# Nine fewer matmuls in the first batch of a sliding-window attention and mixer kernel

## The chip, the cores and the metric

One core of a Trainium2 chip. The metric is device time in microseconds (us) of one execution of the kernel.

## The reference

```python
scores = scale * np.matmul(q, k.transpose(0, 1, 3, 2))   # 8 batches, 8 heads, 576 tokens, 64 wide
rel = pos[:, None] - pos[None, :]
mask = (rel >= 0) & (rel < 64)                           # causal, window of 64
attn = softmax(np.where(mask, scores, -1e9))
x = np.matmul(attn, v)                                   # then (8, 576, 512)
h = x.T @ U @ V                                          # low-rank token mixing, rank 32
u = x + h.T
out = u + np.maximum(u @ w_ch1, 0.0) @ w_ch2             # channel MLP, 512 -> 2048 -> 512
```

## The kernel before

The attention of batch b + 1 is placed into slots between the MLP's matmuls of the chunk before, to keep TensorE without a pause (in the trace of before it is busy 219.98 of the 220.00 us from 60 to 280). Batch 0 has nothing to hide behind: its attention is the prologue, and its variant is called `spare`. There the mask is added before the scores by a matmul of the identity with a bias of 0 or -30000, and the scores are summed on top.

```python
def SC(j):                                   # scores of head pair j
    def f():
        if j not in sbank:
            masked(j)                        # spare: mask bias into both PSUM banks
        sc = sbank[j]
        banks = [sc[:, g, :] for g in range(2)]
        scores(banks, 0, j, 0, 0, 2)         # keys of block 0 with queries of blocks 0 and 1
        scores(banks, 0, j, 1, 0, 1)         # keys of block 1 with queries of block 0
        for u in range(1, NB - 1):
            scores(banks, u, j, u, u, 2 if u < NB - 2 else 1, last=(u >= NB - 3))
        ...                                  # exponential on ScalarE

opened = []
def idle_turns(n):                           # matmuls whose result nobody reads
    cols = P if opened else CH
    bank(1)
    for _ in range(n * (CH // cols)):
        nc.tensor.matmul(bank(0)[:, 0:cols], idle[:, 0:P], idle[:, 0:cols],
                         start=not opened, stop=not opened)
...
turn_over(62, 96)                            # warm-up: 62 unread matmuls of 96 columns
...
order = "K0 K1 B0 B1 Q0 Q1 S0 K2 S1 K3 B2 Q2 Q3 S2 B3 S3 L0 B4 S4 L1"
...                                          # B: mask bias, S: scores, L: first values
load_rest()
a["R"]()
shift_high(0, nc.scalar.copy, 2)
shift_low(0, nc.scalar.copy, 2)
a["idle"](1)
a["PV"][2]()                                 # values product that waits for GpSimd's copies of v
...
for f in [a["U"][NT - 1]] + a["X3"] + a["HT"]:
    f()                                      # psh of 256 columns, then hh; MLP (psA) follows
```

Names in the profile: `psA` and `psU` are the MLP's two products, `psh`/`hh` the low-rank one, `xr` and `xw` values products, `low` the first scores of a later batch, `kr`/`qr` loaded k and q, `kf`/`qf` transposed k and q, `vB` the copy of v shifted by 64 rows. From batch 2 on, k and q are transposed by DMA (SyncE's queue), five tiles of each.

The softmax here doesn't subtract the row's maximum and nothing guards it: scores larger than these inputs give would overflow.

## Time and profile before

| | before |
|---|---|
| median time, first 3 runs | 310.14 us (309.88 to 310.33) |
| span of the profiled run, granted clock | 308.6 us, 1.00 |
| TensorE busy | 302.1 us, 98% |
| first product of the MLP (psA) | 22.02 us |
| sixth instruction packet | 51.81 us |
| last transposed q of batch 2: lands, is used | 67.06, 67.59 us |

From psA on, TensorE is busy without a gap in this trace up to the last product: 11.98 of 12.00 us from 22 to 34, 26.00 of 26.00 from 34 to 60, 219.98 of 220.00 from 60 to 280, 25.07 of 25.07 from 280 to 305.07. So the span is psA's start, plus a fixed amount of work, plus whatever TensorE must wait for after psA. TensorE's position is compared instruction by instruction with this trace, and the difference is called its lead (negative: ahead of this trace). The page sums its chain up so:

```profile
PE 93%; DMA 3%; POOL 2%; issue 1%; DVE 0%; POOLq 0%
```

Two transposes of SyncE's queue, from its timeline in the kernel before (columns: start, length, engine, line, operation):

```profile
55.93 1.57 SPq L307 DMA_TRANSPOSE qf<-qr  x1
57.61 1.21 SPq L307 DMA_TRANSPOSE kf<-kr  x1
```

The second begins 0.11 us after the first ends (57.50 and 57.61). The first stays 1.57 us where its neighbours stay 1.21.

### The profile page before, as it was taken

The page shows a single profiled execution, that of the slowest core. Times are in us where ns is not written, and L with a number is a line of the kernel's source. Part 1 is how long each engine was busy: PE and PEld are TensorE (multiplying, and loading weights), DVE is VectorE, ACT ScalarE, POOL GpSimd, SP SyncE. Part 2 cuts the span into 40 slices and gives each one's busy share as a digit, 9 for nine tenths or more (in the row PEclk, how much of TensorE's full clock was granted, in tenths as well). Part 3 has the DMA queues.
Part 4 walks back from the last instruction along what each step waited for, and adds up shares of the span by engine and source line. Part 5 has one row for each costly group of instructions (what it writes and reads, how often), then busy time and mean ns, then how long its engine had stood idle before and what let it go on. Part 6 is the DMA issues. An engine that isn't in the chain of part 4 may idle for free.

```text
span 308.6 us, 6947 instructions
## 1 busy us (share of the span) xinstructions
PE 302.1 (98%) x2883; PEld 146.4 (47%) x2883; DVE 174.2 (56%) x336; ACT 106.0 (34%) x169; POOL 102.1 (33%) x136
## 2 busy tenths in 40 slices
PE   7989999999999999999999999999999999999995
PEld 7543454545445544454445444544454444444443
DVE  4585467537848763777467755766576542116012
ACT  2745670358008510552064205430443004101500
POOL 8693264195069519417541725000000000000000
PEclk9999999999999999999999999999999999999999
DMA  7999999999999999999999999955100464010011
GB/s 100 169 208 209 206 172 149 148 139 148 148 108 154 126 158 148 195 161 163 175 176 131 176 175 151 155 111 136 71 2 0 106 229 162 34 68 36 0 68 68
DMA packets 158671, 40.39 MB, mean 131 GB/s; under 512 B 147216, under 2 KB 153616, under 8 KB 158640
## 3 DMA queue, kind: packets, MB, share of 16 engines
q0 software_dynamic: 104720, 18.88, 84.8%
q1 hardware_dynamic: 53920, 21.08, 39.3%
q8 instruction: 22, 0.36, 0.5%
q14 instruction: 9, 0.07, 0.1%
HBM read 37.97 MB, written 9.44 MB: 154 GB/s over the span
## 4 chain that ended last, share of the span: by engine, by line
PE 93%; DMA 3%; POOL 2%; issue 1%; DVE 0%; POOLq 0%
PE psA L766 41%; PE psU L790 41%; DMA vA<-in_v_dram 3%; PE sc L348 3%; PE xw L410 2%; PE psv L661 1%; PE pshh L534 1%; PE tpg L284 0%; POOL qr L121 0%; PE low L348 0%; PE psh L534 0%; POOL vB L153 0%; PE tpu L695 0%; PE xr L410 0%; POOL kr L121 0%
## 5 line engine op out<-in xcount | busy, mean ns | idle before, releaser
L766 PE MATMUL psA<-uTc,w1b 128*128 128x512 bf16 (+1 forms) x580 | 131.0, 378 | 0.3 <-DVE uTc L636 0.3
L790 PE MATMUL psU<-w2b,c 128*128 128x512 bf16 (+2 forms) x592 | 128.4, 374 | 0.0
L790 PEld LDWEIGHTS <-c 128*128 128x128 bf16 x592 | 56.1, 98 | 66.4 <-issue 2.9
L766 PEld LDWEIGHTS <-w1b 128*128 128x128 bf16 x580 | 54.0, 98 | 64.4 <-issue 2.6
L778 ACT ACTIVATE c<-psA 128x512 bf16<-128x512 f32 x84 | 50.1, 597 | 80.5 <-PE psA L766 80.2
L776 DVE TENSOR_SCALAR c<-psA 128x512 bf16<-128x512 f32 x60 | 41.4, 690 | 38.5 <-PE psA L766 38.5
L803 DVE TENSOR_TENSOR osb<-psU,un 128x512 f32<-128x512 f32 (+2 forms) x29 | 19.5, 671 | 51.2 <-PE psU L790 51.2
L368 ACT ACTIVATE pts<-sc 128x1024 bf16<-128x1024 f32 x32 | 31.3, 1030 | 2.8 <-PE sc L348 2.8
L139 POOL DMA_DIRECT2D vA<-in_v_dram x32 | 28.3, 904 | 11.5 <-DMA w1b<-in_moe_w_ch_dram 3.0
L676 DVE TENSOR_TENSOR un<-psv,xs 128x512 bf16<-128x512 f32 (+3 forms) x48 | 25.8, 594 | 6.6 <-PE psv L661 6.5
L130 POOL DMA_DIRECT2D qr<-in_q_dram x30 | 26.6, 887 | 7.0 <-DMA w2b<-in_moe_w_ch_dram 2.9
L130 POOL DMA_DIRECT2D kr<-in_k_dram x30 | 26.3, 876 | 5.0 <-PE psA L766 2.0
L401 ACT ACTIVATE ptl<-low 128x256 bf16<-128x256 f32 x6 | 2.3, 383 | 64.9 <-PE high L348 64.9
L374 DVE TENSOR_TENSOR pts<-pts,maskA 128x1024 bf16<-128x1024 bf16 x28 | 19.0, 683 | 2.2 <-ACT pts L368 2.2
L501 DVE TENSOR_TENSOR xs<-xw,rcw 128x896 bf16<-128x896 f32 x14 | 15.3, 1092 | 0.5
L965 POOL COPY held<-qf 1x1 bf16<-1x1 bf16 x5 | 0.9, 178 | 44.2 <-DMA qf<-qr 44.2
L348 PEld LDWEIGHTS <-kf 64*64 64x64 bf16 x704 | 9.8, 107 | 7.6 <-issue 7.3
L348 PE MATMUL sc<-qf,kf 64*64 64x128 bf16 (+1 forms) x608 | 11.5, 212 | 0.5 <-DVE qf L301 0.3
L410 PEld LDWEIGHTS <-pts 128*64 128x64 bf16 x512 | 10.0, 110 | 3.7 <-issue 3.1
L139 POOL DMA_DIRECT2D vB<-in_v_dram x8 | 7.2, 896 | 5.6 <-DMA qr<-in_q_dram 2.4
L803 DVE TENSOR_TENSOR late<-psU,un 128x512 f32<-128x512 f32 x8 | 5.4, 686 | 6.1 <-PE psU L790 6.1
L410 PE MATMUL xw<-vA,pts 128*64 128x65 bf16 x217 | 8.5, 195 | 0.0
(125 smaller groups left out, 177.1 us busy)
## 6 DMA issues: line engine op xcount, KB each, us to landing
out_dram<-osb SPq DMA_DIRECT2D x27, 256.0 KB, 2.3
vA<-in_v_dram POOLq DMA_DIRECT2D x32, 128.0 KB, 9.6
kr<-in_k_dram POOLq DMA_DIRECT2D x24, 128.0 KB, 7.6
qr<-in_q_dram POOLq DMA_DIRECT2D x24, 128.0 KB, 7.5
w2b<-in_moe_w_ch_dram POOLq DMA_DIRECT2D x4, 512.0 KB, 15.6
out_dram<-late SPq DMA_DIRECT2D x8, 256.0 KB, 3.0
vB<-in_v_dram POOLq DMA_DIRECT2D x8, 128.0 KB, 11.3
w1b<-in_moe_w_ch_dram POOLq DMA_DIRECT2D x2, 512.0 KB, 10.9
```

The source lines that it names most:

```text
L130: nc.gpsimd.dma_start(out=dst[0:rows, t, :, :], in_=src[b, :, t * P : t * P + rows, :].rearrange("h p d -> p h d"),)
L139: nc.gpsimd.dma_start(out=dst[:, :, 0:D], in_=v[b, :, lo : lo + P, :].rearrange("h p d -> p h d"))
L348: nc.tensor.matmul(sc[g][r0 : r0 + W, col * W : (col + n) * W], keys_of(j, u, rs), queries_of(j, blk, n, rs), start=not spare, stop=last o ...
L368: nc.scalar.activation(out=dst, in_=sc[:], func=ACT.Exp, scale=scale)
L374: nc.vector.tensor_tensor(out=dst, in0=dst, in1=maskA.rearrange("p g n w -> p g (n w)"), op=ALU.mult)
L410: nc.tensor.matmul(dst, pts[:, h // 2, h % 2, blk, :] if blk < NB - 1 else ptl[:, h // 2, h % 2, :], rhs, start=True, stop=True,)
L676: nc.vector.tensor_tensor(out=u_tiles[g][rs, cs], in0=ps[0][n][rs], in1=x[rs, t, :, :].rearrange("p h d -> p (h d)")[:, cs], op=ALU.add,)
L766: nc.tensor.matmul(ps[i][:, ts.start * P : ts.stop * P], w1b[:, dc, i * P : (i + 1) * P], uTc[:, ts, dc, :], start=(dc == 0), stop=(dc == ...
L776: nc.vector.tensor_relu(out=c1[i][:], in_=ps[i][:])
L778: nc.scalar.activation(out=c1[i][:], in_=ps[i][:], func=ACT.Relu)
L790: nc.tensor.matmul(acc[t][:, lo:hi], c1[i][:, t * P : (t + 1) * P], w2b[:, i, lo:hi], start=(i == 0), stop=(i == NFC - 1),)
L803: nc.vector.tensor_tensor(out=osb[:, lo:hi], in0=acc[t][:, lo:hi], in1=u_tiles[g][:, lo:hi], op=ALU.add,)
```

## The change

Its intent: remove TensorE work from the prologue. The product of block 1's keys with block 0's queries is masked anyway: its columns hold -30000 from the bias, with or without it. It goes for batch 0 (two matmuls in each of four head pairs), and the unread matmul before the values product goes too.

```diff
                 scores(banks, 0, j, 0, 0, 2)
-                scores(banks, 0, j, 1, 0, 1)
+                if not spare:
+                    scores(banks, 0, j, 1, 0, 1)
...
-        opened = []
-
-        def idle_turns(n):
-            cols = P if opened else CH
-            ... (body cut)
         def XT(t, dcs):
             def f():
-                opened.append(t)
...
-            pcs["idle"] = idle_turns
...
     shift_low(0, nc.scalar.copy, 2)
-    a["idle"](1)
     a["PV"][2]()
```

More of the change, by code (lines that the diff above doesn't have):

```diff
@@ L590, in bank @@
             return ua[dc]
-        opened = []
-        def idle_turns(n):
-            cols = P if opened else CH
-            bank(1)
-            for _ in range(n * (CH // cols)):
-                nc.tensor.matmul(
-                    bank(0)[:, 0:cols],
-                    idle[:, 0:P],
-                    idle[:, 0:cols],
-                    start=not opened,
-                    stop=not opened,
-                )
         def XT(t, dcs):
             def f():
-                opened.append(t)
                 for dc in dcs:
```

## The prediction

> **What bounds the kernel now.** I read the page first. Its busy table and its chain that ended last say the same thing: TensorE.
>
> ```profile
> span 308.6 us, 6947 instructions
> PE 302.1 (98%) x2883; PEld 146.4 (47%) x2883; DVE 174.2 (56%) x336; ACT 106.0 (34%) x169; POOL 102.1 (33%) x136
> q8 instruction: 22, 0.36, 0.5%
> ```
>
> So anything that lets TensorE start its dense part earlier is worth its full length, unless something later waits; anything that shortens work before a wait is worth nothing. The nine removed matmuls all lie in batch 0, before the first product of the MLP (psA) at 22.02 us. I therefore asked for busy time by stretch: from 22 to 34 us TensorE is busy 11.98 of 12.00, from 34 to 60 it is 26.00 of 26.00, from 60 to 280 it is 219.98 of 220.00, each at a granted clock of 1.00. Before 22 us it has holes. The question is which of the holes swallow the saving. The chain in order of time, from 6 to 22 us, answers that:
>
> ```profile
> 5.29 0.88 POOL vA L139
> 6.17 8.05 DMA vA<-in_v_dram
> 14.22 0.05 issue
> 14.27 0.61 POOL vB L153
> 14.88 0.06 issue
> 14.94 0.62 POOL vB L150
> 15.56 0.06 issue
> 15.61 0.62 POOL vB L153
> 16.24 0.04 issue
> 16.28 0.45 PE xr L410 x16
> ...
> 19.53 0.32 PE psh L534 x2
> 19.85 0.31 issue
> 20.16 0.32 PE psh L543 x4
> 20.49 0.02 issue
> 20.51 0.43 DVE hh L575
> ```
>
> (Columns: start, length, what.) Until 16.28 us the chain is not TensorE at all: a load of v lands at 14.22, GpSimd makes three shifted copies of it, and only then may TensorE begin the values product of 16.28. After that TensorE carries the chain, with one hole named "issue", 19.85 to 20.16. The last view is TensorE's timeline around the removed idle matmul (L598) and that hole:
>
> ```profile
> 15.70 0.39 PE L598 MATMUL uam<-idle 128*128 128x512 bf16 x1
> 16.28 0.19 PE L410 MATMUL xr<-vB,pts 128*64 128x65 bf16 x1 [0.19 <-POOL vB L153]
> ...
> 20.16 0.29 PE L543 MATMUL psh<-xs,ub 128*32 128x256 bf16 x4 [0.31 <-issue]
> 20.99 0.39 PE L626 MATMUL uam<-vrep,hh 64*128 64x256 bf16 x4 [0.20 <-DVE hh L575]
> ```
>
> [...] a 512-column mask matmul is followed by its like after 0.22 us but by a 64-column transpose after 0.31 us, so a switch costs some 0.09 us, and L598 sits between two. [...] The page above has 22 instruction packets of 0.36 MB together, 16 KB each[...]; that matters below.
>
> **The change part by part.**
>
> 1. Scores. In each of four head pairs, two 64x64 matmuls go, with their weight loads. Eighteen matmuls of such a group take 0.35 us from their start to the next group's (9.60 to 9.95), so about 20 ns each: 8 x 20 = 0.16 us. Two groups stand before 11 us, two before 14.1 us. All are before the 16.28 wait, which a DMA landing and GpSimd set. ScalarE's exponentials may start 0.04 us earlier, but the third product's inputs and the v copies do not. On the path: 0.
> 2. The idle matmul: 0.22 us of streaming and two mode switches of 0.09 us, about 0.4 us. It also stands before 16.28. On the path: 0. The order of instructions shows that only its two waits go with it, and that the first transposing matmul into that PSUM bank now carries the wait for VectorE itself; that matmul runs at 16.66 and the wait was met by 15.70, so nothing new is waited for.
> 3. Nothing else moves: in ScalarE, VectorE, GpSimd and DMA queues the order and waits are the same. TensorE's stream is 18 rows shorter (nine loads, nine matmuls).
>
> By parts 1 and 2 the gain is 0 although about 0.55 us of TensorE work goes. Part 3 is where I expect what little there is. The hole before L543 has no cause in the data: its weight load waits for nothing and still starts only at 20.16, and the matmul's input from VectorE was signalled at 19.56 (semaphore records of the trace). By the 0.21 us that 512 columns take, it could have started at 19.68, so the hole is 0.48 us. In the trace an instruction packet moves from 17.78 to 18.72 us. I take the hole for the end of an instruction line that was late [...]; the profile does not say so, it is an inference. If so, the line ends at a fixed row, and 18 rows fewer before it move the end from the first weight load of L543 to the second product of L626. That product waits for VectorE anyway: with L543 at 19.68 the two halves of hh are cast from 20.03, the first signalled at about 20.46 instead of 20.95, and the late line, there at 20.16 or a little later, hides under it. Then psA starts at 22.02 - 0.48 = 21.54.
>
> What of 0.48 us survives? I compared landing times with first use. The second q load of batch 1 lands at 33.18 and is used at 33.93: enough. The fourth piece of w2b lands at 47.97 (issued at 36.01, 12.0 us to landing) and its first product starts at 48.29. With a few hundredths for the signal, TensorE can gain only 48.29 - 48.02 = 0.27 us there. Behind it nothing binds closer: the last transposed q of batch 2 lands at 67.06, used at 67.59. So if the hole moves, the gain is about 0.27 us; if not, 0.
>
> **Rivals.**
>
> - All removed work counts: 0.55 us, 309.6. For it: TensorE is 98% busy. Against it: the chain at 16.28 belongs to GpSimd and a load.
> - Nothing counts, the hole stays in front of L543 (it has another cause, or the late line is not at a fixed row): 310.1.
> - The hole moves but lands worse, say the instruction packet now comes later, or the first packet (10.83 us, 0.95 us long), behind which one of the sixteen shares of each v tile lands a microsecond late (13.15 against 12.18 for the rest), shifts relative to those loads. Later: plus 0.3, 310.4. If it moved out of the way of the loads, GpSimd's chain could start earlier, by up to a microsecond: 309.2. The packet would have to move by more than 2 us for that; 12 rows will not do it.
> - [...]
>
> **Range and chances.** I give the moved hole 60%, no effect 25%, the rest 15%. Around the best guess of 0.27 us that makes a mean gain close to 0.2 us: 310.14 - 0.2, so 309.9 us. Three runs of the kernel before span 309.88 to 310.33, so a median may sit 0.2 us off. The range 309.3 to 310.5 holds all but [...] the lucky DMA shift. 2% would be 6.2 us, more than ten times the removed work[...].
>
> **What would show it.** Right: the values product after GpSimd's copy still starts at about 16.28, now after a longer wait for GpSimd; the hole before the 256-column psh products is gone or below 0.1 us; hh is cast about 0.4 us earlier; psA starts near 21.5; a new wait of some 0.2 us for w2b appears near 48. Wrong: the 16.28 moves earlier (then TensorE's own work was on the path, or the v load landed earlier), the hole stays at 20.16, or a granted clock below 1.00 or 512-column matmuls longer than 0.39 us appear after 16 us.

The forecast's sum: 310.14 minus a mean gain close to 0.2 us (0.27 us for the moved hole, which had 60%) gives 309.9, with 309.3 to 310.5 around it. The granted clock was 0.999 to 1.00 in all five runs of the changed kernel.

A switch, or mode switch, is the step from one tile shape to another, and its 0.09 us is an estimate: the 0.31 us from the start of a 512-column mask matmul to that of a transpose (7.96 and 11.35 us in the trace of before) less the 0.22 us to one of its like. The removed 0.55 us is an estimate too, from 0.16 us for the score products and about 0.4 for the idle matmul (0.22 and two switches). An instruction line is the stretch of TensorE's rows that one instruction packet is taken to bring; that a hole stands at its end, at a fixed row, was an inference, which before_minus9 and before_minus4 test below. Why a line should be late is not shown.

## The result, and the profile after

| | before | after |
|---|---|---|
| median (range), 5 runs each | 310.31 us (309.88 to 310.58) | 310.59 us (310.28 to 310.91) |
| ratio after/before, 95% | | 1.0012 (0.9998 to 1.0026) |

A ratio is the mean time of one kernel's runs over that of the other's of the same rounds, so not quite the ratio of the medians quoted. The time of 310.59 is 0.09 us above the predicted range.

The page of the changed kernel: its span, its busy time, and the summary of its chain.

```profile
span 308.9 us, 6908 instructions
PE 299.5 (97%) x2853; PEld 145.7 (47%) x2874; DVE 175.4 (57%) x336; ACT 106.0 (34%) x169; POOL 102.3 (33%) x136
PE 90%; DMA 4%; POOL 2%; DVE 2%; issue 1%; POOLq 0%; SPq 0%
```

The counts hold a trap: the matmuls fall by 30 and the weight loads by 9. Nine were removed; the remaining 21 are matmul records that the trace lost, so the 2.6 us less of busy TensorE are mostly not real. What can be trusted is the chain: DMA and VectorE have taken 3% that TensorE had.

The chain in order of time, before the MLP (start, length, what; the lines answer to those that the prediction quotes):

```profile
15.80 0.62 POOL vB L153
16.43 0.04 issue
16.47 0.45 PE xr L411 x16
...
19.68 0.32 PE psh L535 x2
20.01 0.14 PE psh L544 x4
20.17 0.43 DVE hh L576
...
21.68 1.02 PE psA L751 x4
```

The values product still follows GpSimd's third copy, now 0.19 us later because the load of v landed at 14.41 instead of 14.22. But the "issue" line in front of the 256-column psh is gone, and psA starts at 21.68, 0.34 us ahead. That part went as predicted. Then the lead is lost. TensorE's waits list (us in total, times, longest) names where:

```profile
PE xr L411 <- POOL vB L153: 0.8, 1, 0.8
...
PE xw L411 <- DVE vB L153: 0.2, 1, 0.2
...
PE low L348 <- DMA qf<-qr: 0.2, 1, 0.2
```

The first is the predicted longer wait for GpSimd. The other two are new, and both lie behind psA:

1. At 67.5 us the first scores of batch 2 (`low`) wait for the last transposed q. It landed at 67.06 before and lands at 67.44 now, although TensorE arrives earlier. SyncE's timeline in the changed kernel shows where it was held up:

```profile
55.55 2.65 SPq L307 DMA_TRANSPOSE qf<-qr  x1
58.30 1.21 SPq L307 DMA_TRANSPOSE kf<-kr  x1
```

This transpose began 0.38 us earlier than before and stayed 2.65 us instead of 1.57, so the next begins 0.69 later. In the DMA records, the sixth instruction packet (16 KB) moves at 55.84, taking 1.57 us; before it moved at 51.81 in 0.97 us. Beside it, the last q load of batch 2 lands at 58.71 instead of 57.65; of its sixteen shares one came at 57.36, the other fifteen at 58.34 to 58.71. The lead shrinks from -0.34 to -0.11.

2. At 101 us a values product of batch 3 waits for VectorE's copy of v. In the chain of the changed kernel:

```profile
100.43 0.60 DVE c L761
101.03 0.93 DVE vB L153 x2
101.97 0.04 issue
102.01 0.39 PE xw L411 x13
```

The second of the two copies takes 0.80 us by its record; in the kernel before both together fitted into 0.52:

```profile
101.06 0.52 DVE L153 COPY vB<-vA 64x520 bf16<-64x520 bf16 x2
```

The lead goes from -0.11 to +0.26. Another 0.05 us slips in later: the last product starts at 305.38 against 305.07. The account of the trace closes: -0.34 + 0.23 + 0.37 + 0.05 = +0.31 us, which is the 0.3 by which the spans differ.

### The profile page after: what moved, and what is told of

It reads as the page before. It is cut to its first block, busy times and chain, and to the rows that moved or that the text cites. A ratio compares the mean times of both kernels' runs of the same rounds, so it can differ in the third digit from the quotient of the medians. Undisturbed runs are those within 1.5% of the kernel's fastest.

```text
span 308.9 us, 6908 instructions
## 1 busy us (share of the span) xinstructions
PE 299.5 (97%) x2853; PEld 145.7 (47%) x2874; DVE 175.4 (57%) x336; ACT 106.0 (34%) x169; POOL 102.3 (33%) x136
## 4 chain that ended last, share of the span: by engine, by line
PE 90%; DMA 4%; POOL 2%; DVE 2%; issue 1%; POOLq 0%; SPq 0%
PE psU L775 40%; PE psA L751 39%; DMA vA<-in_v_dram 3%; PE sc L348 3%; PE xw L411 2%; DMA qf<-qr 2%; PE psv L647 1%; PE pshh L535 1%; DVE c L761 1%; PE tpg L284 0%; POOL qr L121 0%; PE low L348 0%; PE psh L535 0%; POOL vB L153 0%; PE tpu L681 0%
## 5 line engine op out<-in xcount | busy, mean ns | idle before, releaser
L775 PE MATMUL psU<-w2b,c 128*128 128x512 bf16 (+2 forms) x573 | 126.9, 373 | 1.2 <-issue 0.3
```

The costliest lines, as they stand in the source:

```text
L775: nc.tensor.matmul(acc[t][:, lo:hi], c1[i][:, t * P : (t + 1) * P], w2b[:, i, lo:hi], start=(i == 0), stop=(i == NFC - 1),)
```

## The experiments

**The theory**: the shorter instruction stream moves the sixth instruction packet onto batch 2's last loads (this takes part of the lead), and the copy at 101 takes the rest. **Rivals**: the losses are chance, in both kernels alike; or the score products and the idle matmul matter for themselves, by their work or the waits they carried.

All traces side by side. "Packet" is the start of the sixth instruction packet, "q load" the landing of the last q load of batch 2, "qf" that of the last transposed q, "low" the start of its first use; "wait" the wait there; "last" the start of the last product. Rows are TensorE instructions, a weight load and a matmul each one. (That these packets carry TensorE's instructions is an inference: the trace of before holds 22 of them and 5766 loads and matmuls, 262 for each, and the stops found below under before_minus9 lie 256 rows apart.) The list of waits leaves out those under 0.15 us.

| trace | early rows | psA | packet | q load | qf | low | wait | last |
|---|---|---|---|---|---|---|---|---|
| before | 0 | 22.02 | 51.81 | 57.65 | 67.06 | 67.59 | - | 305.07 |
| before_again | 0 | 21.56 | 52.12 | 57.67 | 66.95 | 67.13 | - | 304.91 |
| idle_only | -2 | 21.59 | 51.90 | 57.20 | 66.42 | 67.22 | - | 305.00 |
| before_minus4 | -8 | 22.18 | 51.57 | 57.48 | 66.15 | 67.75 | - | 306.04 |
| scores_only | -16 | 21.66 | 55.85 | 58.37 | 67.17 | 67.38 | - | 305.20 |
| after | -18 | 21.68 | 55.84 | 58.71 | 67.44 | 67.49 | 0.2 | 305.38 |
| after_again | -18 | 21.80 | 55.89 | 59.06 | 68.26 | 68.30 | 0.6 | 305.98 |
| after_third | -18 | 21.64 | 55.84 | 58.80 | 68.01 | 68.05 | 0.8 | 306.12 |
| before_minus9 | -18 | 22.64 | 56.61 | 57.43 | 67.97 | 68.21 | - | 305.78 |
| after_plus9 | 0 | 22.28 | 51.88 | 57.37 | 66.67 | 67.86 | - | 306.41 |
| plus9_pv9 | 0 | 21.93 | 51.77 | 57.27 | 66.75 | 67.50 | - | 305.03 |
| after_late9 | -18, then 0 | 21.53 | 51.64 | 57.44 | 66.67 | 67.10 | - | 305.01 |
| late9_pv9 | -18, then 0 | 22.78 | 51.76 | 57.71 | 66.53 | 68.35 | - | 306.07 |
| late9_pv9_again | -18, then 0 | 21.51 | 51.64 | 57.55 | 67.08 | 67.27 | - | 305.10 |

### before_again: the kernel before, unchanged

> The kernel before, unchanged, traced a second time, to see what differs between two runs of one kernel. Theory (instruction line): the hole ahead of the 256-column psh products stands at about 20.2 us again, psA starts within 0.25 us of 22.0, and no product waits at 67.6 or 101.7 us. Rival (the later waits come and go by chance): a wait for the transposed q near 67.6 or for the DVE copy of v near 101.7 shows here too. Time ratio 1.000 within 0.001.

Measured: 310.06 us (309.81 to 310.61), ratio 0.998 (0.9961 to 0.9998) against other runs of the identical kernel in the same rounds, which came out at 310.64 (309.86 to 311.4). The interval leaves out 1 although nothing was changed: a difference of 0.2% is not resolved here, even where the interval says so. The trace is the more telling part. The hole before the 256-column psh is not there: psh starts at 19.64 and psA at 21.56. The kernel before has that head start by itself in this trace; of the two traces of the unchanged kernel one has the hole and one has not. And the copy of v at 101 cost this kernel 0.25 us too. VectorE's timeline of this run:

```profile
100.81 0.68 DVE L153 COPY vB<-vA 64x520 bf16<-64x520 bf16 x1
```

So the wait at 101 does not belong to the change.

### after_again and after_third: the changed kernel, unchanged

> The changed kernel, unchanged, traced a second time. Theory: no hole ahead of the psh products again, psA near 21.7, and the waits near 67.5 (transposed q) and 101.7 (DVE copy of v) are both there again, so that the end comes 0.2 to 0.4 us later than before; the first belongs to the sixth instruction packet falling at 55.8 instead of 51.8. Rival (chance): at least one of the two waits is missing and the span is then 0.2 to 0.7 us shorter. Time ratio 1.0005 to 1.0015 by the theory, 0.999 to 1.001 by chance.

> The changed kernel a third time, beside the two above on one chip. Theory: packet at 55.8, q load landing at 58.4 to 59.1, last product 305.2 or later, and time 0.2 to 0.6 us above after_late9. Rival: a third trace without the late q load, and a time that cannot be told from after_late9.

Measured: 310.69 us (310.42 to 311.18), ratio 0.9997 (0.9977 to 1.0016), and 310.74 us (310.24 to 311.32), ratio 1.0007 (0.999 to 1.0024). The wait at 67.5 is in both traces, longer than in the first. TensorE's waits lists, first of after_again, then of after_third:

```profile
PE low L348 <- DMA qf<-qr: 0.6, 1, 0.6
```

```profile
PE low L348 <- DMA qf<-qr: 0.8, 1, 0.8
```

With the packet at 55.84 to 55.89 in all three, the wait goes with the changed kernel in each of its traces, which chance would hardly do. Its size is not fixed (0.2 to 0.8 us), and none of it was won back by the end of these traces. But the traced executions of after_again and after_third (311.18 and 311.32 us) were the slowest of their six, so they are not typical of the kernel's time.

### scores_only and idle_only: each half of the change alone

```diff
  scores_only: kernel before, and
-                scores(banks, 0, j, 1, 0, 1)
+                if not spare:
+                    scores(banks, 0, j, 1, 0, 1)
  idle_only: kernel before, and
-    a["idle"](1)
```

> Only the eight score products go, the idle matmul stays: 16 rows fewer ahead of the psh products. Theory (instruction line at a fixed row): the line now ends inside the first HT pair, where VectorE is waited for anyway, so the hole ahead of the 256-column psh products is gone and psA starts near 21.6 to 21.8. Rival (the idle matmul's removal made the hole vanish[...]): the hole stays and psA starts near 22.0.

> Only the idle matmul goes, the score products stay: 2 rows fewer ahead of the psh products. Theory (line at a fixed row): the line ends one load and one product later, inside the group of four psh products, so three of the four wait as before, hh is cast as late as before, and psA starts near 22.0. Rival (the idle matmul was the cause): no hole, psA near 21.7.

Measured: scores_only 310.28 us (309.85 to 310.61), ratio 0.9985 (0.9967 to 1.0003); idle_only 310.69 us (310.21 to 311.42), ratio 1.0 (0.998 to 1.0019). In idle_only psA started at 21.59; I had expected about 22.0, the hole staying in front of psh. It was a miss, and before_again explains it: there was no hole to keep. The packets separate cleanly: 16 rows fewer put the sixth packet at 55.85 and the q load at 58.37, two rows fewer leave them at 51.90 and 57.20. In scores_only the last transposed q still came 0.21 us before its use, so no wait; at 67.17 it landed later than in any trace with the early packet (67.08 at most), and the margin is a matter of tenths. The times cannot rank the halves.

### before_minus9 and before_minus4: fewer rows, all products kept

To take rows away without touching the change, the warm-up was given fewer and wider matmuls, with nearly the same number of columns (62 x 96 = 5952, 53 x 112 = 5936, 58 x 102 = 5916).

```diff
  before_minus9: kernel before, and
-    turn_over(62, 96)
+    turn_over(53, 112)
  before_minus4: kernel before, and
-    turn_over(62, 96)
+    turn_over(58, 102)
```

> The kernel before with 53 warm-up matmuls of 112 columns in place of 62 of 96 (the same 5 us of warm-up): all nine products of the change stay, but TensorE's stream is 18 rows shorter ahead of everything, as in the changed kernel. Theory (row count moves the sixth instruction packet into the last q load of batch 2): the packet falls at 55.8 +- 0.2 us instead of 52, that q load lands at 58.4 to 59.1 instead of 57.2 to 57.7, the last transposed q at 67.2 to 68.3, and the end comes as late as in the changed kernel: last product at 305.2 to 306.0, time 310.3 to 310.8. Rival (the removed products themselves, or chance): packet at 52, last product at 304.9 to 305.1, time 310.0 to 310.3.

> The kernel before with 58 warm-up matmuls of 102 columns: 8 rows fewer. Where the step lies between 2 rows (packet at 51.9) and 16 rows (55.85). Theory: the packet falls either near 52 or near 55.8, or between, later the fewer rows[...]. Rival: no relation between the row count and the packet.

Measured: before_minus9 310.98 us (310.58 to 311.47), ratio 1.0028 (1.0016 to 1.0041); before_minus4 one run, 311.26 us. Eighteen rows fewer moved the packet to 56.61 (expected 55.8), without any of the change's edits; the q load of batch 2 was on time though (57.43), which I had not expected, and yet the last transposed q came at 67.97, since two transposes stayed long in SyncE's queue (1.71 and 1.95 us). Eight rows fewer left it at 51.57. So the number of rows moves the packet, and the way from the packet to the transposed q is not always the q load.

The loss of time has its place elsewhere, and it is the clearest picture of a stop that the data do not explain. TensorE's timeline in before_minus9:

```profile
13.77 0.34 PE L348 MATMUL sc<-qf,kf 64*64 64x128 bf16 x10
15.03 0.30 PE L348 MATMUL sc<-qf,kf 64*64 64x128 bf16 x8 [0.92 <-issue]
```

In the middle of a group of 18 equal products, with nothing in the data to wait for, TensorE stops for 0.92 us. In before_minus4 it stops in the same score group for 0.74, after five products instead of ten. Counted in rows, with TensorE's few drain and semaphore rows, both stop after the same one, row 449 of its stream, whatever stands there; the hole of the first trace of before comes after row 705, exactly 256 rows further. TensorE went on 2.4 to 2.65 us after the start of the instruction packet before it (17.78 and 20.16; 12.40 and 15.03; 11.86 and 14.51). That fits the prediction's inference, that this hole is the end of an instruction line whose successor comes late, though no trace shows the line itself. What was wrong was to count on it: the hole differs from run to run (0.31 us in the first trace of before, none in before_again). The hole explains most of the loss in before_minus9 (psA 0.62 us late, the last product 0.71), but not in before_minus4: there psA is only 0.16 us late, and 0.36 us go at the copy of 101 and 0.37 near 175 (the place found below in late9_pv9_again).

### after_plus9 and plus9_pv9: the change, with the rows given back at the start

```diff
  after_plus9: changed kernel, and
-    turn_over(62, 96)
+    turn_over(71, 84)
  plus9_pv9: after_plus9, and
-    PLACE_3 = {**PLACE, "SV": [5, 5, 6, 6], "V": [16], ...}
+    PLACE_3 = {**PLACE, "SV": [5, 5, 6, 6], "PV": [9], "V": [16], ...}
```

The second edit places the values product of batch 3 one slot later, so that the copy at 101 has time.

> The changed kernel with 71 warm-up matmuls of 84 columns in place of 62 of 96: the nine products are gone, but the stream has the row count of the kernel before. Theory: the packet is back at 52 us, the q load lands at 57.2 to 57.7, the last product starts at 304.9 to 305.1, time 310.0 to 310.3. Rival: packet or not, the end is as in the changed kernel, 310.5 to 310.8.

> after_plus9, and the values products of batch 3 one slot (0.86 us) later, so that they no longer wait for VectorE's shifted copies of v near 101 us. Theory (that wait eats what head start is left, 0.14 to 0.37 us in the five traces that have one): no product waits near 101, the last product starts at 304.6 to 304.8, time 309.7 to 310.1, faster than both kernels by 0.1%. Rival (another wait behind it takes its place): 305.0 and 310.2.

Measured: after_plus9 312.52 us (311.62 to 313.51), ratio 1.0085 (1.0069 to 1.01); plus9_pv9 310.29 us (310.13 to 310.65), ratio 1.0004 (0.9992 to 1.0016). The packet went back to 51.88 and 51.77, the q load to 57.37 and 57.27, and no wait was left at 67.5: that half hit. The times missed: in both traces the second q load of batch 0 was late (12.37 and 12.02 us, against 11.42 in the changed kernel). The rows at the start had also moved the first packet, to 9.92 and 9.90 us from 10.51; that this delayed the load is not shown, since late9_pv9 below has that load later still, at 12.87, with its first packet at 10.47. TensorE's waits list of after_plus9:

```profile
PE tpg L284 <- DMA qr<-in_q_dram: 0.9, 1, 0.9
PE xw L411 <- DVE vB L153: 0.6, 1, 0.6
```

after_plus9 also ran at a granted clock of 0.989 to 0.998 (the others at 0.998 or more, with few exceptions): its two runs at 0.989 took 313.51 and 312.60 us, the traced one at 0.998 took 311.62. So its 2 us are not all explained by these waits. In plus9_pv9 the wait at 101 is gone, as its edit meant it to be.

### after_late9, late9_pv9 and late9_pv9_again: the rows given back late

The cleaner way: leave the prologue as changed, and give the 18 rows back after its last matmul, as nine small unread ones.

```diff
  after_late9: changed kernel, and
     for f in [a["U"][NT - 1]] + a["X3"] + a["HT"]:
         f()
+    gap = psum["spare"].tile([P, CH], FP32, name="gap", tag="spare")
+    for _ in range(9):
+        nc.tensor.matmul(gap[:, 0:32], idle[:, 0:P], idle[:, 0:32], start=True, stop=True)
  late9_pv9 and late9_pv9_again: after_late9, and "PV": [9] in PLACE_3 as above
```

> The changed kernel with nine unread matmuls of 32 columns put behind batch 0's last products, where TensorE waits 0.6 us for VectorE anyway: the stream before them keeps the 18 rows fewer, the stream behind them has the row count of the kernel before. Theory (the sixth instruction packet, moved by the row count, delays the last q load of batch 2): no hole ahead of the psh products and psA near 21.7 as in the changed kernel, but the packet is back at 51.5 to 52.3 us, the q load lands at 57.2 to 57.8, no wait for the transposed q near 67.4; last product at 304.8 to 305.1, 0.3 to 0.6 us before the changed kernel of the same call; time 310.0 to 310.3. Rival (the loss is chance): packet or not, same time as the changed kernel within 0.1 us.

> after_late9, and batch 3's values products one slot later, past VectorE's shifted copies of v near 101 us. Theory: neither of the two later waits is left, so the head start of 0.3 to 0.45 us at psA lasts to the end: last product at 304.6 to 304.75, time 309.7 to 310.0, 0.1% faster than the kernel before. Rival (a further wait takes it): 305.0, time as after_late9.

> The same kernel as late9_pv9 (the changed kernel, nine unread small matmuls given back after the stretch, values of batch 3 one slot later), run again because its first trace fell on a late second q load of batch 0. Theory (the time lost between psA and the end is the q wait at 67.5 and the values copy at 101.5, both taken away here): in a trace in which the q load of batch 0 is on time, psA starts at about 21.6, there is no wait at the first score product of batch 2 and none for a DVE copy at 101, the last product starts at 304.5 to 304.8, and the median is 309.7 to 310.0, ratio 0.996 to 0.999. Rival (what is won there is waited for again later, or the time is set by chance at the start): last product at 305.0 or later, median 310.3 to 310.7, ratio 0.999 to 1.001.

Measured: after_late9 310.40 us (310.21 to 311.46), ratio 1.0002 (0.9984 to 1.0019). The 0.6 us of the expectation run from the start of batch 0's last product to that of psA (21.10 to 21.68 in the trace of the changed kernel, of which the profile counts 0.31 as idle). Here psA is at 21.53, the packet at 51.64, the q load at 57.44, and there is no wait at 67.5. That is the changed kernel with its work still removed, and only the number of rows restored; the packet, the load and the wait all went back. Together with before_minus9, which has fewer rows and every product, this shows that the row count moves the packet and, with it, the last transposed q: it landed at 67.17 us or later in all five traces with the late packet and at 67.08 or earlier in the nine others. Whether TensorE then waits also depends on its lead (scores_only has the late packet and no wait). The step in between, a packet that slows the loads and transposes beside it, is not shown; it is an inference from their times (in the changed kernel's trace a packet of 1.57 us at 55.84, a transpose of 2.65 us from 55.55, the q load 1.06 us later than before). SyncE's timeline of this run, the same two transposes:

```profile
55.75 1.31 SPq L307 DMA_TRANSPOSE qf<-qr  x1
57.16 1.21 SPq L307 DMA_TRANSPOSE kf<-kr  x1
```

Of its lead of -0.49 the copy of v near 101 (0.65 us long) took 0.22, and the products near 175 took another 0.16; the last product came at 305.01.

late9_pv9, which has both waits taken away: 310.63 us (309.71 to 311.68), ratio 0.9999 (0.9976 to 1.0022). Its trace fell on a late second q load of batch 0 (a wait of 1.4 us), psA was at 22.78, and it says only that no wait followed at 67 or 101. So it was run again: 310.26 us (309.89 to 310.37), ratio 0.9987 (0.9972 to 1.0002). Now psA was at 21.51, a lead of -0.51. The first 0.19 us of it went where the prediction had set its limit: the fourth piece of w2b landed at 47.92 and its first product began at 47.96. The rest, -0.33, passed 67.5 and 101 whole. I expected the last product at 304.5 to 304.8; it came at 305.10. The lead met one more place. At 174.7 us the products with `hh` (psv) wait for a chain of VectorE operations, in which one copy took 0.90 us instead of the 0.41 of the kernel before. VectorE's timelines, first of late9_pv9_again, then of before:

```profile
172.62 0.90 DVE L567 COPY other<-part 32x512 f32<-32x512 f32 x1
```

```profile
172.94 0.41 DVE L566 COPY other<-part 32x512 f32<-32x512 f32 x1
```

The third of the psv products, which waits for the end of that chain, began at 175.19 against 175.06, and -0.33 had become +0.03 when the psU after it went on. The longer copy began 0.25 us into a DMA issue of GpSimd (172.37 to 173.27); in the kernel before it began when such an issue had 0.03 us left. Being early is what put it there; the section on the prediction comes back to this. So the rival's expectation came true: take two waits away, and what is won is waited for again later. No version was shown faster than the kernel before.

## Why the prediction was wrong

It gave 309.9 us, 309.3 to 310.5; the result was 310.59, and 310.69 and 310.74 in later rounds.

- **Score products and idle matmul, on the path 0** (steps 1 and 2): right. The values product still waits for GpSimd's copies, 0.8 us instead of 0.2, and begins when the load of v lets it.
- **The hole before psh moves and is hidden** (step 3): right in the trace, psA at 21.68 for a predicted 21.54. But the premise was one trace. before_again has psA at 21.56 with all nine matmuls in place. The whole predicted gain of 0.27 us was measured against a hole that the kernel before does not always have.
- **The limit of 0.27 us at w2b**: right in kind, its size not fixed. In the changed kernel's first trace the piece landed at 47.82 us, 0.15 earlier than before, and no wait arose near 48. In four other traces it did: 0.19 us were lost there in late9_pv9_again (landing 47.92), 0.17 in after_again (48.29), 0.14 in scores_only (48.03), 0.05 in idle_only (47.87).
- **"Behind it nothing binds closer: the last transposed q of batch 2 lands at 67.06, used at 67.59."** This is the step that failed, at two places: the transposed q took 0.23 us of the lead and a copy that the list of landings could not contain took 0.37 (next point), so that the trace ends 0.31 us behind instead of 0.27 ahead. For the transposed q, the step compares a landing time of the old kernel with a use of the new one, as if landings stayed. The 18 rows that I took to move one line's end to a harmless place also moved the sixth packet, from 51.8 to 55.8 us, and in the same trace the last q load of batch 2 landed at 58.71 instead of 57.65 and one transpose stayed 2.65 us instead of 1.57. The last transposed q came at 67.44 to 68.26, and TensorE waited in all three traces of the changed kernel. after_late9, which only restores the row count, has none of it. I had a later packet in a rival ("the hole moves but lands worse, say the instruction packet now comes later", plus 0.3 us, 310.4) but looked for it only near the first packets.
- **The copy at 101**: not considered at all. It cost 0.37 us in the changed kernel's trace, and 0.25 in before_again, so it does not belong to the change; it makes a head start worthless. All 14 traces together show which copies stay long. They hold 182 VectorE copies of two kinds (126 of v, 64x520; 56 like the one at 172.62, 32x512). Of these 138 took their plain 0.27 to 0.29 or 0.41 to 0.42 us. The other 44 (up to 0.83 us for v) all began when a DMA issue of GpSimd had been running for at least 0.24 us, and each ended a nearly fixed time after that issue ended: 0.08 to 0.12 us (v), 0.24 to 0.25 us (32x512). The 0.80 us copy ran from 101.16 to 101.96, beside an issue from 100.81 to 101.84. Copies begun in the first 0.23 us of an issue, or with less than about 0.2 us of it left, took their plain time, such as the one at 99.56 beside an issue from 99.47 to 100.28 (0.28 us). So a copy's length depends on where in an issue it begins, which a shift of a few tenths changes. This is a regularity without an exception, found by going through the traces; no run moved GpSimd's issues to test it, and why a copy stays long beside an issue is not shown.
- **The range**: 310.5 as the upper end rested on three runs from 309.88 to 310.33. With 53 runs of the kernel before in all rounds, 309.76 to 311.62, the mean is 310.44; the 17 runs of the changed kernel have a mean of 310.71. The range was too narrow for noise alone, and the 310.14 from which it counted lies 0.30 below that mean.

One slip in its working changes nothing: by its step 1, two groups stand before 11 us, so 8 rows go before the first packet and not the 12 of its third rival (that packet came at 10.51 us instead of 10.83).

What stays open. Why the packet moves by 4 us: when it starts in the first trace of before (51.81), TensorE stands at about row 1474, and the next 18 rows, small low-rank products, take it only to 52.3. Why the q load stayed on time in before_minus9. And whether the changed kernel is slower at all: its three ratios are 1.0012, 0.9997 and 1.0007, each with 1 in its interval, and two sets of runs of the identical kernel differed by 0.2%. That the wait at 67.5 comes with the change is shown by the traces; that it costs time in the median is not: the traces without it ended at 304.91 at best, 0.16 us ahead of the first trace of before, since w2b and the copies took what was left of their lead.

## What to carry to other kernels

Work removed in front of a wait gained nothing here (the wait for GpSimd grew from 0.2 to 0.8 us), and the removed rows still counted: with 18 fewer the sixth instruction packet came 4 us later, and a wait of 0.2 to 0.8 us came with it, for an estimated 0.55 us of work removed. A lead won early must be followed to the end past every later landing and copy, each with its new time and not its old one: of the four places met here (48, 67.5, 101 and 175 us) the prediction counted on only the first. Before a gap of a few tenths of a us is built into a prediction, run the unchanged kernel a second time and see whether the gap is still there.
